# Rolling the TensorE program of a decode layer into a loop, with fixed slots for the K and V loads

## Chip, cores, metric

The kernel runs on one core of a Trainium2 chip. The metric is device microseconds of one execution. All comparisons below are between runs in the fast state, each with runs of the kernel before on the same chip. A ratio is the mean time of one kernel's fast runs over the mean of the other's from the same rounds, so it is not quite the ratio of the medians that are quoted beside it. Beside the experiments the kernel before measured 295.97 to 296.06 us, so medians of different rounds can be compared too.

## The reference

One decode step (one new token, batch 2) of a transformer layer in bf16: layernorm, attention over the last 2048 positions of a K and V cache, out-projection, residual, layernorm, gated FFN, residual.

```python
# D = 640, 32 heads of 192, window W = 2048, FFN width 1536   (cut)
q = (x @ wq).reshape(B, 1, 32, 192).transpose(0, 2, 1, 3)
k = k_cache[:, :, Sk - W:, :]
v = v_cache[:, :, Sk - W:, :]
p = softmax(einsum("bhqd,bhkd->bhqk", q, k) * 192 ** -0.5)
o = einsum("bhqk,bhkd->bhqd", p, v)
h = x + o.reshape(B, 1, 6144) @ wo
out = h + (gelu(ln(h) @ w_gate) * (ln(h) @ w_up)) @ w_down
```

There is almost no reuse: every byte of K and V is used once. The work is 16 groups (4 heads of one batch each), and a group needs one K load and one V load of 3.15 MB each.

## The kernel before

A small recorder collects operations with the tiles that they read and write, works out the waits, and emits one straight-line program for each engine. Loads go into a ring of five slots of 24,576 bytes per partition. They are issued in order, each as soon as the data that it overwrites has been used. For each group TensorE transposes K (12 chunks of 4 transposes), VectorE and ScalarE copy the chunks into `ktr`, and then come scores, softmax and PV.

```python
ring = sb("ring", [128, RING // 2], BF16)          # RING = 5 * 24576
ktr = sb("ktr", [128, 2, 3, 4096], BF16)           # two buffers of transposed K
rq = sb("rq", [128, NG, 6, 16], BF16)              # masked q of all 16 groups

def load(key, nbytes, src, shape):                 # ring position
    if pos[0] + nbytes > RING:
        pos[0] = 0
    off, i = pos[0], pos[1]
    pos[0], pos[1] = off + nbytes, i + 1
    queue.append((key, off, nbytes, src, shape, i))
...
for g in range(NG):                                # order of loads
    if g > 0 and g + 1 < NG:
        load_k(g + 1)
    load_v(g)
    if g % 4 == 3 and g < NG - 5:
        load_wo(g // 4)
load_wo(2); load_wo(3); load_ffn()
...
for g in range(NG):                                # unrolled: 16 groups   (cut)
    transposes(g + 1, 0)
    e_columns(g)
    if J is not None: o_columns(J)                 # every fourth group
    transposes(g + 1, 1)
    if J is not None and J < 2: oproj(J)
    pv(g)
    scores(g + 1)
    softmax(g + 1)
o_rows(3); oproj(2); o_columns(3); oproj(3)        # then layernorm and FFN
```

## Time and profile before

| | before |
|---|---|
| median of 4 runs | 295.99 us (295.89 to 296.05) |
| span of the profiled run | 294.3 us |
| data queue, share of 16 DMA engines | 97.5% |
| TensorE busy | 68% |
| instruction packets (queue q8) | 17, 0.28 MB |

The page's slices (40 equal parts of the span) and its DMA queue table (packets, MB, share of the span of 16 engines):

```profile
PE   2473658848687298849494695858597858586864
DMA  7999999999999999999999999999999999999992
GB/s 268 431 429 445 449 428 426 428 426 424 426 418 433 423 438 431 428 424 438 433 416 446 430 424 423 428 428 430 428 426 431 430 438 423 428 431 411 429 407 113
q1 hardware_dynamic: 6632, 122.29, 97.5%
q8 instruction: 17, 0.28, 0.4%
```

The DMA row is 9 (90% or more) everywhere but in the first and last slice: the loads never pause. TensorE works in bursts.

The waits table (who waited for whom, us in total, times, longest us), and TensorE's timeline for one group (start, us, what):

```profile
PE tps L478 <- DMA ring<-in_A_k_cache_dram: 47.3, 15, 6.9
```

```profile
238.60 4.51 PE L478 MATMUL tps<-identf,ring 128*128 128x128 f32 x24 [3.21 <-DMA ring<-in_A_k_cache_dram]
242.94 0.28 PE L560 MATMUL m<-sel,eexp 128*128 128x64 bf16 x4
243.06 2.82 PE L478 MATMUL tps<-identf,ring 128*128 128x128 f32 x24
245.90 1.49 PE L576 MATMUL ops<-ring,ering 128*32 128x384 bf16 x32
247.21 1.53 PE L534 MATMUL sps<-ktr,rq 128*16 128x512 bf16 x24
249.81 0.18 PE L547 MATMUL m<-mrhs,pm 128*128 128x16 bf16 x1 [1.08 <-DVE mrhs L326]
```

From K's landing at 238.60 to the last matmul at 249.99 a group takes TensorE 11.4 us; the stream brings the next pair of K and V after 14.6 us. So TensorE has about 3 us to spare in a group.

The chain of waits in order of time (start, us, what), its end:

```profile
247.81 29.22 DMA ring<-in_A_wo_dram
...
277.06 0.73 PE m L627 x5
...
291.63 0.33 DVE yrow L748
```

The last piece of `wo` lands at 277.0 us. After it comes a tail of 17.3 us in which out-projection, layernorm and FFN follow one another, while the FFN weights are still arriving. The time is therefore the landing of `wo` plus the tail.

### The profile page before, as it was taken

To read this page: it belongs to the slowest core of one execution; us is meant where nothing else is said; L and a number is where in the kernel's file an instruction comes from. 1 tells how busy PE (TensorE), PEld (TensorE's weight loads), DVE (VectorE), ACT (ScalarE), POOL (GpSimd) and SP (SyncE) were. 2 spreads that over 40 slices of the span, in tenths; PEclk is the share of its full clock that TensorE was granted. 3 is DMA by queue.
4 is the path that set the end of the run, shared out by engine and by line. 5 is a ranking of instruction groups with operands and counts; after the bars stand their busy time and mean duration, and the time that the engine had idled before them with its cause. 6 is when DMAs were issued, how large, how long until landed. Compare 5 with 4: busy or idle time off the path is not lost.

```text
span 294.3 us, 4896 instructions
## 1 busy us (share of the span) xinstructions
PE 198.8 (68%) x2141; PEld 152.4 (52%) x2141; DVE 130.4 (44%) x326; ACT 95.6 (32%) x119; POOL 2.7 (1%) x19
## 2 busy tenths in 40 slices
PE   2473658848687298849494695858597858586864
PEld 1451256728374285637382675655575555553432
DVE  5950366614447054525264343626266526252332
ACT  2150134624332153516151333425254334341000
POOL 3000000000000000000000000000000000000000
PEclk9996579996979589989779697979689979795555
DMA  7999999999999999999999999999999999999992
GB/s 268 431 429 445 449 428 426 428 426 424 426 418 433 423 438 431 428 424 438 433 416 446 430 424 423 428 428 430 428 426 431 430 438 423 428 431 411 429 407 113
DMA packets 6665, 122.61 MB, mean 417 GB/s; under 512 B 754, under 2 KB 756, under 8 KB 1396
## 3 DMA queue, kind: packets, MB, share of 16 engines
q1 hardware_dynamic: 6632, 122.29, 97.5%
q8 instruction: 17, 0.28, 0.4%
q14 instruction: 4, 0.03, 0.0%
q10 hardware_dynamic: 12, 0.00, 0.0%
HBM read 122.29 MB, written 0.00 MB: 416 GB/s over the span
## 4 chain that ended last, share of the span: by engine, by line
DMA 69%; PE 24%; DVE 4%; SPq 1%; issue 1%; ACT 0%; DVEq 0%; ACTq 0%
DMA ring<-in_A_k_cache_dram 50%; PE tps L478 17%; DMA ring<-in_A_wo_dram 10%; DMA ring<-in_A_wq_dram 10%; PE ops L576 1%; DVE rq L330 1%; PE m L627 1%; SPq L271 1%; PE sps L696 1%; PE m L742 1%; PE m L609 1%; PE ops L696 1%; PE tps L707 1%; PE tps L500 1%; PE m L646 0%
## 5 line engine op out<-in xcount | busy, mean ns | idle before, releaser
L478 PE MATMUL tps<-identf,ring 128*128 128x128 f32 x768 | 115.0, 318 | 48.4 <-DMA ring<-in_A_k_cache_dram 47.3
L478 PEld LDWEIGHTS tps<-identf,ring 128*128 128x128 f32 x768 | 106.6, 167 | 51.6 <-DMA ring<-in_A_k_cache_dram 48.7
L487 ACT ACTIVATE ktr<-tps 128x1024 bf16<-128x1024 bf16 x80 | 79.3, 1023 | 88.5 <-PE tps L478 86.9
L490 DVE COPY ktr<-tps 128x1024 bf16<-128x1024 bf16 x112 | 74.2, 688 | 75.7 <-PE tps L478 75.0
L551 ACT ACTIVATE eexp<-sm,nm 128x512 bf16<-128x512 f32 x16 | 11.5, 721 | 64.7 <-DVE nm L549 64.7
L576 PE MATMUL ops<-ring,ering 128*32 128x384 bf16 x512 | 25.0, 339 | 3.6 <-DMA ring<-in_A_v_cache_dram 3.4
L534 PE MATMUL sps<-ktr,rq 128*16 128x512 bf16 x384 | 26.0, 404 | 0.4 <-DVE rq L330 0.4
L540 DVE CUSTOM_DVE_ANT_1 sm<-sps,mska 128x512 f32<-128x512 f32 x16 | 11.1, 691 | 34.1 <-PE sps L534 34.1
L576 PEld LDWEIGHTS ops<-ring,ering 128*32 128x32 bf16 x512 | 12.7, 99 | 12.6 <-DMA ring<-in_A_v_cache_dram 5.6
L534 PEld LDWEIGHTS sps<-ktr,rq 128*16 128x16 bf16 x384 | 9.6, 90 | 11.4 <-issue 2.2
L547 PEld LDWEIGHTS m<-mrhs,pm 128*128 128x128 bf16 x16 | 1.5, 96 | 25.0 <-DVE mrhs L326 25.0
L547 PE MATMUL m<-mrhs,pm 128*128 128x16 bf16 x16 | 2.9, 183 | 16.9 <-DVE mrhs L326 16.9
L500 PE MATMUL tps<-ring,xnT 128*32 128x384 bf16 x80 | 5.7, 444 | 7.6 <-DMA ring<-in_A_wq_dram 7.6
L330 DVE TENSOR_TENSOR rq<-ops,mask 128x96 bf16<-128x96 f32 x16 | 2.7, 250 | 14.6 <-PE ops L518 14.6
L500 PEld LDWEIGHTS tps<-ring,xnT 128*32 128x32 bf16 x80 | 2.4, 119 | 10.4 <-DMA ring<-in_A_wq_dram 8.6
L330 DVE TENSOR_TENSOR ering<-m,mask 128x256 bf16<-128x256 f32 x16 | 6.7, 419 | 2.2 <-PE m L560 2.0
L382 ACT ACTIVATE lt<-m,eps_t 128x2 f32<-128x2 f32 x2 | 0.5, 262 | 20.2 <-PE m L380 20.2
L627 PE MATMUL m<-ring,ot 128*2 128x320 bf16 x96 | 5.7, 379 | 0.3 <-DVE ot L613 0.3
L560 PE MATMUL m<-sel,eexp 128*128 128x64 bf16 x64 | 4.7, 198 | 1.2 <-ACT eexp L551 1.2
L330 DVE TENSOR_TENSOR orow<-m,wm 128x1536 bf16<-128x1536 f32 x3 | 5.3, 1750 | 0.0
L560 PEld LDWEIGHTS m<-sel,eexp 128*128 128x128 bf16 x64 | 4.3, 103 | 1.5 <-DVE nm L549 1.3
L586 DVE COPY osb<-ops 128x192 f32<-128x192 f32 x8 | 2.5, 354 | 5.8 <-PE ops L576 5.8
(112 smaller groups left out, 82.1 us busy)
## 6 DMA issues: line engine op xcount, KB each, us to landing
ring<-in_A_k_cache_dram SPq DMA_DIRECT2D x16, 3072.0 KB, 26.3
ring<-in_A_v_cache_dram SPq DMA_DIRECT2D x16, 3072.0 KB, 29.7
ring<-in_A_wq_dram SPq DMA_DIRECT2D x2, 3072.0 KB, 21.1
ring<-in_A_wo_dram SPq DMA_DIRECT2D x3, 1920.0 KB, 32.2
ring<-in_B_w_gate_dram SPq DMA_DIRECT2D x1, 1920.0 KB, 33.3
ring<-in_B_w_up_dram SPq DMA_DIRECT2D x1, 1920.0 KB, 25.7
ring<-in_B_w_down_dram SPq DMA_DIRECT2D x4, 480.0 KB, 27.6
ring<-in_A_wq_dram SPq DMA_DIRECT2D x1, 1536.0 KB, 28.1
```

The source lines that it names most:

```text
L330: return lambda e: e.tensor_tensor(out=out, in0=a, in1=b, op=op)
L478: ins = e.transpose(tps[bi][:, 128 * u:128 * (u + 1)], kv[:, off:off + 128], identf[:, :])
L487: act(lambda e, dst=dst, bv=bv: e.activation(out=dst, in_=bv, func=ACT.Copy), W=[("kt", slot, n)], X=[("t", bi)])
L490: dve(lambda e, dst=dst, bv=bv: e.tensor_copy(dst, bv), W=[("kt", slot, n)], X=[("t", bi)])
L500: ins = e.matmul(tps[0][32 * r:32 * (r + 1), 0:384], lhsT=xnT[:, c, 32 * J:32 * (J + 1)], rhs=wq[:, c - c0, 1536 * J + 384 * r:1536 * J + ...
L534: ins = e.matmul(sps[32 * ch:32 * ch + 16, :], lhsT=rq[:, g, k, :], rhs=ktr[:, g % 2, k // 2, 1024 * ch + k % 2:1024 * (ch + 1):2], start= ...
L540: dve(lambda e: e.tensor_tensor_reduce(out=sm[:, :].rearrange("p (u x) -> p u x", u=4), in0=sps[:, :].rearrange("p (u x) -> p u x", u=4), ...
L551: act(lambda e: e.activation(out=eexp[:, :], in_=sm[:, :], func=ACT.Exp, bias=nm[:, 0:1], scale=1.0, accum_out=zr[:, g // 4 % 2, g % 4:g % ...
L560: ins = e.matmul(o, lhsT=eexp[:, 128 * u:128 * (u + 1)], rhs=sel64[:, :], start=True, stop=True)
L576: ins = e.matmul(ops_[32 * r:32 * (r + 1), 0:384], lhsT=ering[:, g % 4, t, :], rhs=vv[:, 384 * t:384 * (t + 1)], start=(g % 4 == 0 and t < 4),
L627: ins = e.matmul(m1[32 * r:32 * r + 2, 192:512], lhsT=ot[:, J % 2, kk, :], rhs=wo[:, kk - k0, 320 * h:320 * (h + 1)], start=(kk == 1 or J ...
L696: ins = e.matmul(bank[32 * r:32 * r + 2, 0:384], lhsT=hnT[:, c, :], rhs=wv[:, c, 384 * r:384 * (r + 1)], start=(c == 0), stop=(c == NC5 - ...
```

## The change

It rolls TensorE's program into a loop of 4 trips of 4 groups. The loop as written uses the same addresses in each trip, so the ring gives way to fixed slots (four for K, two for V), the transposed K keeps one buffer, and the masked q of four groups is held at a time and made by GpSimd. A wait inside the loop compares a semaphore with `S * i + a`, where `i` is the trip in a register. The core of the diff (the recorder's bookkeeping is cut):

```diff
-RING = 5 * 24576
+SLOT = 24576
+RING = 6 * SLOT
+K_AT = (0, SLOT, 2 * SLOT, 3 * SLOT)
+V_AT = (4 * SLOT, 5 * SLOT)
+WO_AT = (3 * SLOT, 3 * SLOT, 2 * SLOT, 0)
...
-        ktr = sb("ktr", [128, 2, 3, 4096], BF16)
+        ktr = sb("ktr", [128, 3, 4096], BF16)
-        rq = sb("rq", [128, NG, 6, 16], BF16)
+        rq = sb("rq", [128, 4, 6, 16], BF16)
+        qs = sb("qs", [128, 384], BF16)
...
-            for g in range(NG):            # at the start, on VectorE
-                dve(tt(rq[:, g, ...], ...))
+            dve(lambda e: e.tensor_copy(qs[:, :], ops_[:, 0:384]), W=["qs"], X=["o"])
+            for g in range(4):
+                q_masked(g)                # pool(tt(rq[:, g % 4, ...], ...))
...
             pe(fn, R=[("rq", g % 4)] + [("kt", n) for n in range(12)], X=["s"])   # scores(g)
+            if g + 4 < NG:
+                q_masked(g + 4)
...
+        with eng.Fori(0, trips) as i:
+            ...
+                    for n, o, waits in sorted(bodies.pop(item), key=lambda q: q[0]):
+                        self.emit_one(o, eng, sems, [(key, S * i + a if S else a) for key, a, S in waits])
...
-            P.emit("pe", e, sems)
+            P.emit_loop(e, sems, 4, ["a0", (0, None, ["oc"]), "a1", (0, 3, ["op"]), "a2", "b0", "b1", "b2", "c0", "c1", "c2",
+                                     (None, 3, ["d0", "d1", "d2"])])
```

Bytes and order of the loads stay as they were.

## The prediction

> **What bounds the kernel now.** The DMA stream. The page's slices show DMA share 0.9 or more from the second to the 39th; the queue table gives the data queue 97.5% of 16 engines' span for 122.29 MB. In the windows view each 14.6 us stretch from 44 to 248 us has DMA share 0.99 to 1.01 and about 430 GB/s, with PE busy 7.5 to 12.8 us, mean 10.47. One K and one V (2 x 3.15 MB) take those 14.6 us. TensorE follows: the waits table has it idle 47.3 us for K, 15 times. In the chain of waits the last piece of wo lands at 277.0 us; then out-projection, layernorm and FFN run 17.3 us in latency, while the last FFN weights arrive just in time.

> **What the change does to that.** Bytes, load order and tail stay. Five rotating slots become six fixed ones. By the release conditions, V of group g+2 now needs pv(g) instead of the transposes just before it (1.5 us later), and wo0 and wo1 wait for the transposes of groups 3 and 7 (before, wo0 went out at 61.4 us). At each of these moments two to three transfers of 7.3 us are still queued, 15 to 20 us. The single transposed-K buffer should cost nothing: in TensorE's order scores(g) already precede the transposes of g+1.

> **Costs added on TensorE.** About 20 waits per group become register waits. A stand-alone semaphore instruction on TensorE's queue took 51 ns in this trace; at an estimated two or three such steps per wait that is 2 to 3 us per group, partly hidden behind queued matmuls and evictions. A regular group needs 11.6 us from K's landing to its last small matmul (238.6 to 250.0 in the timeline), one with an out-projection 13.4 (164.1 to 177.6), against 14.6 or more of stream: mostly absorbed. [...] three back-edges and one skip, spread over 250 us, should be recovered from the slack.

> **Gains.** Sixteen DVE multiplies (2.7 us) leave the start; GpSimd does one per group, well ahead of need. The first softmax starts 2 us earlier, but the stream isn't waiting there. Instruction traffic is 0.28 MB, 0.4% in the queue table. If rolling removed three quarters of it, some engines would finish 1 us earlier; if each trip refetches its body, nothing is gained.

> **Critical part.** Almost none: the stream stays saturated, so I expect 295.8 us, 8 in 10 between 294.0 and 298.0. Chances: faster by over 2% 0.01, within 2% 0.95, slower 0.04.

> **What would show it.** DMA share 0.9 or more in all slices from the second to the 39th; TensorE's total wait for K falling from 47 to 15 to 40 us; the last wo piece landing at 277 plus or minus 1.5 us, tail about 17 us; TensorE's busy time unchanged within 3%; the rq multiplies on POOL.

> **What would make it wrong.** Register waits that cost much more than 3 us per group, or that drain the queue before each transposed chunk, so that TensorE needs over 14.6 us per group: then DMA slices drop, the queue's own waits on V slots grow, and the time rises by 16 times the excess. Or back-edge stalls over 15 us, longer than the queued transfers. Or a wait merged over trips that is stricter than the unrolled program's and delays a V or wo load.

The forecast comes to 295.8 us, the 295.99 us measured before with almost nothing taken off. That the back-edges should be recovered from the slack was my estimate. So were the two or three steps in each register wait; the 51 ns for one of them are from the trace.

## The result and the profile after

The changed kernel takes 294.80 us (294.61 to 294.94, 4 runs) against 295.99 us; ratio 0.996, interval 0.9943 to 0.9977. It is 1.2 us faster: clear of noise, well within 2%.

The same parts of the page after the change:

```profile
PE   2573586858677298849493597659696869666764
DMA  7999999999999999999999999999999999999993
GB/s 279 436 427 433 431 440 435 430 425 430 425 420 438 430 433 427 430 430 430 430 421 436 430 430 430 430 430 433 430 430 430 430 430 430 430 430 426 430 406 125
q1 hardware_dynamic: 6632, 122.29, 97.8%
q8 instruction: 7, 0.11, 0.2%
```

The stream is as full as before, and in the second half it is steadier: 430 GB/s in nearly every slice, where before it wandered between 411 and 446. The instruction queue moved 7 packets in place of 17.

The waits table, TensorE's timeline for the same group, and the end of the chain:

```profile
PE tps L549 <- DMA ring<-in_A_k_cache_dram: 45.5, 14, 7.4
```

```profile
237.25 5.38 PE L549 MATMUL tps<-identf,ring 128*128 128x128 f32 x24 [1.84 <-DMA ring<-in_A_k_cache_dram]
242.43 0.42 PE L636 MATMUL m<-sel,eexp 128*128 128x64 bf16 x4
242.66 3.10 PE L549 MATMUL tps<-identf,ring 128*128 128x128 f32 x24
245.69 1.49 PE L652 MATMUL ops<-ring,ering 128*32 128x384 bf16 x32
247.00 1.53 PE L608 MATMUL sps<-ktr,rq 128*16 128x512 bf16 x24
249.61 0.18 PE L623 MATMUL m<-mrhs,pm 128*128 128x16 bf16 x1 [1.08 <-DVE mrhs L398]
```

```profile
248.90 26.84 DMA ring<-in_A_wo_dram
275.78 0.73 PE m L703 x7
...
290.29 0.32 DVE yrow L830
```

The whole gain has arrived when `wo` lands: 275.8 us in place of 277.0. The tail is 293.0 - 275.8 = 17.2 us, as before. Past the first 24 transposes, whose 5.38 us in place of 4.51 may be no more than the granted clock (0.50 in that stretch, 0.62 before), the group is 0.28 us longer (242.63 to 249.79, before 243.11 to 249.99). So the loop's bookkeeping hardly shows. Counted in the trace, TensorE's queue ran 196 register ALU operations (median 32 ns), 19 fused register operations and 19 compare-and-branch (median 77 ns, longest 349 ns) and one move, together 9.7 us of recorded durations in the whole run, or 0.6 us a group; 8.9 of the 9.7 us lay while a matmul was running.

The question is why the same bytes in the same order arrive 1.2 us sooner.

### The profile page after: what moved, and what is told of

It reads as the page before. It is cut to its first block, busy times and chain, and to the rows that moved or that the text cites. A ratio compares the mean times of both kernels' runs of the same rounds, so it can differ in the third digit from the quotient of the medians.

```text
span 293.0 us, 5065 instructions
## 1 busy us (share of the span) xinstructions
PE 198.8 (68%) x2141; PEld 153.0 (52%) x2141; DVE 128.5 (44%) x311; ACT 95.7 (33%) x119; POOL 8.4 (3%) x35
## 3 DMA queue, kind: packets, MB, share of 16 engines
q1 hardware_dynamic: 6632, 122.29, 97.8%
HBM read 122.29 MB, written 0.00 MB: 417 GB/s over the span
## 4 chain that ended last, share of the span: by engine, by line
DMA 72%; PE 23%; SPq 2%; DVE 2%; issue 1%; ACT 0%
DMA ring<-in_A_k_cache_dram 54%; PE tps L549 16%; DMA ring<-in_A_wq_dram 10%; DMA ring<-in_A_wo_dram 9%; SPq L342 2%; PE ops L652 1%; PE m L703 1%; PE m L824 1%; PE sps L778 1%; PE ops L778 1%; PE m L685 1%; PE tps L789 1%; PE tps L571 1%; PE m L722 0%; DVE grow L785 0%
## 5 line engine op out<-in xcount | busy, mean ns | idle before, releaser
L549 PE MATMUL tps<-identf,ring 128*128 128x128 f32 x768 | 116.5, 320 | 46.4 <-DMA ring<-in_A_k_cache_dram 45.5
L652 PE MATMUL ops<-ring,ering 128*32 128x384 bf16 x512 | 24.4, 334 | 4.7 <-DMA ring<-in_A_v_cache_dram 4.7
L616 DVE CUSTOM_DVE_ANT_1 sm<-sps,mska 128x512 f32<-128x512 f32 x16 | 11.1, 691 | 34.9 <-PE sps L608 34.9
L402 POOL TENSOR_TENSOR rq<-qs,mask 128x96 bf16<-128x96 bf16 x16 | 5.6, 359 | 195.9 <-PE sps L608 164.9
L594 DVE CAST qs<-ops 128x384 bf16<-128x384 f32 x1 | 0.6, 558 | 14.4 <-PE ops L589 14.4
L636 PE MATMUL m<-sel,eexp 128*128 128x64 bf16 x64 | 5.3, 213 | 1.2 <-ACT eexp L627 1.2
L636 PEld LDWEIGHTS m<-sel,eexp 128*128 128x128 bf16 x64 | 4.9, 114 | 1.7 <-DVE nm L625 1.3
L703 PE MATMUL m<-ring,ot 128*2 128x320 bf16 x96 | 4.9, 338 | 1.1 <-DMA ring<-in_A_wo_dram 1.1
```

What stands on the lines that cost most here:

```text
L402: return lambda e: e.tensor_tensor(out=out, in0=a, in1=b, op=op)
L549: ins = e.transpose(tps[bi][:, 128 * u:128 * (u + 1)], kv[:, off:off + 128], identf[:, :])
L616: dve(lambda e: e.tensor_tensor_reduce(out=sm[:, :].rearrange("p (u x) -> p u x", u=4), in0=sps[:, :].rearrange("p (u x) -> p u x", u=4), ...
L636: ins = e.matmul(o, lhsT=eexp[:, 128 * u:128 * (u + 1)], rhs=sel64[:, :], start=True, stop=True)
L652: ins = e.matmul(ops_[32 * r:32 * (r + 1), 0:384], lhsT=ering[:, g % 4, t, :], rhs=vv[:, 384 * t:384 * (t + 1)], start=(g % 4 == 0 and t < 4),
L703: ins = e.matmul(m1[32 * r:32 * r + 2, 192:512], lhsT=ot[:, kk, :], rhs=wo[:, kk - k0, 320 * h:320 * (h + 1)], start=(kk == 1 or J < 2 and ...
```

## The experiments

Three theories stood at first. Theory I: fewer instruction packets share the DMA engines with the loads. Theory S: the slots and the order of issue do it. Theory M: the start does it, which VectorE's 16 multiplies no longer fill. A fourth, theory L, came after the first batch: the loop changes the timing of TensorE and so of the releases.

### unrolled and unrolled_dvemask: the change without its loop

```diff
-            P.emit_loop(e, sems, 4, [...])
+            P.emit("pe", e, sems)
```

In the second kernel the masks are also VectorE's again, all 16 at the start.

> The changed kernel with its TensorE program unrolled again; the six fixed slots, the single transposed-K buffer and the GpSimd masks stay. Theory I (the gain of 1.2 us comes from fewer instruction packets on the DMA engines: 17 before, 7 after): the instruction queue is back at about 17 packets and 0.28 MB, ratio to the kernel before 0.999 to 1.001, about 296 us. Theory S (the gain comes from the slots, the order of issue or the masks, not from the loop): 7 or 17 packets, but ratio stays at 0.996, about 294.8 us.

> As unrolled, and the masked q made by VectorE for all 16 groups at the start, as before the change: of the change only the fixed slots and the single buffer are left. Theory I: equal to unrolled within 0.3 us, about 296 us. Theory M (the 2.2 us of VectorE work taken from the start shorten the run): unrolled is near 294.8 and this one near 296 us. The first softmax starts about 2 us later than in unrolled in either case.

Measured: 296.16 us (ratio 1.0004, interval 0.999 to 1.0018) and 296.04 us (1.0001, 0.9987 to 1.0014). The queue table of unrolled:

```profile
q1 hardware_dynamic: 6632, 122.29, 97.6%
q8 instruction: 17, 0.28, 0.4%
```

With the loop taken out, the time and the 17 packets are back. Slots, single buffer and masks are together worth nothing that can be measured, so theories S and M fall. The gain belongs to the loop; what in the loop brings it was still open between I and L.

### fill1 and fill2: more instructions on GpSimd, first attempt

```diff
+            def fn(e):
+                for _ in range(363 if g > 3 else 0):      # fill2: 726
+                    e.nop(nofuse=True)
+                return mul(e)
```

> The changed kernel with 363 no-operations on GpSimd ahead of each of its twelve later masks (4356 in all, about 17 blocks of 16 KB of instructions on an engine that has nothing else to do). Theory I: some 17 more instruction packets than the changed kernel's 7, and about 0.12 us for each, so 296 to 297 us. Theories S and M: 294.8 us, since neither slots, TensorE program nor start differ. The masks must still come in time: no wait of the scores for them beyond the first.

> As fill1 with 726 no-operations a time (8712, about 34 blocks). Theory I: twice the excess of fill1 over the changed kernel, 298 to 299 us, if the packets spread over the engines as before. Theories S and M: 294.8 us.

Measured: 294.92 and 294.90 us, q8 still 7 packets and q14, GpSimd's instruction queue, still 3. This says nothing about theory I: the trace shows only 12 semaphore instructions more on GpSimd's queue, so the no-operations were evidently merged at build time and never fetched. The two runs serve as repeats of the changed kernel.

### loop2x8: a loop whose body is twice as long

```diff
-    P.emit_loop(e, sems, 4, ["a0", ..., (None, 3, ["d0", "d1", "d2"])])
+    P.emit_loop(e, sems, 2, ["a00", ..., "d02", "a10", ..., (None, 1, ["d10", "d11", "d12"])])
```

> The changed kernel's loop as 2 trips of 8 groups in place of 4 trips of 4: same slots, masks and matmuls, and a TensorE program of about 2800 instructions (11 blocks of 256) against about 1790 (7 blocks) in the changed kernel and 4270 (17 blocks) in the kernel before. Theory I (instruction packets): 11 packets if the second trip finds its blocks still in TensorE's instruction memory, up to 19 if it fetches them again; time 294.8 plus 0.12 us for each packet over 7, so about 295.3 us with 11 and 296 us with 17 to 19. Theory L (the loop gains by another timing of TensorE and of the releases, not by traffic): 294.8 us whatever the packets.

Measured: 297.57 us (297.49 to 297.83), ratio 1.0053, interval 1.004 to 1.0066: slower than both kernels, by less than 2% but clear of noise.

```profile
q1 hardware_dynamic: 6632, 122.29, 97.0%
q8 instruction: 21, 0.34, 0.5%
```

A block is what one packet of q8 brings: 16,384 bytes in the records of both kernels, and by the program's counts about 256 instructions (about 1790 in the 7 packets of the changed kernel). This program has 11 such blocks, and 21 packets were moved: the second trip fetched most of its body again. The branch back at 158.0 us took 6.0 us, and nine packets followed between 161.5 and 262.5 us. That stall is not the loss: TensorE had to wait for the next K until 165.4 us anyway. The 4-trip program, some 1790 instructions or 7 blocks, moved 7 packets. Five start by 90.4 us, before its first branch back at 93.6, and the next only at 274.8, so its four trips fetched nothing twice. Theory L (294.8 us for any such loop) fails. Theory I has the sign right but not the size: at 0.12 us for each packet, 21 packets should have cost 1.7 us over the changed kernel, and they cost 2.8 us. The number of packets is not the whole story; the next section finds the rest.

### The lag of the slowest engine

Every load of K, V or weights leaves 16 packets of 4 bytes among the records, and 16 dated increments of its semaphore; the page counts 16 DMA engines. What waits for the load starts after the last increment: in the kernel before, those of the K load that TensorE waits for at 238 us run from 235.21 to 238.55 us, and the transposes start at 238.60. I read each increment as one engine's share being done; the records name no engine. The distance from the first to the last of the 16 is the lag of the slowest engine behind the fastest. Worked out from the increments for the last V load (the packets of 4 bytes carry no load's name and mix two loads where the lag is longer than the distance between them):

```
run               q8 packets   of them before        lag at the last   median time, us
                  in all       the last V lands      V load, us
fill1                  7              5                   2.07             294.92
pework3 (below)        7              5                   2.14             294.95
after                  7              5                   2.21             294.80
fill2                  7              5                   2.33             294.90
before                17             14                   3.36             295.99
unrolled              17             14                   3.38             296.16
unrolled_dvemask      17             14                   3.62             296.04
loop2x8               21             18                   4.97             297.57
```

From after to before the lag grows by 1.15 us and the time by 1.19 us; from after to loop2x8 they grow by 2.76 and 2.77 us. One microsecond of lag costs about one microsecond of time here, because what waits for a load starts after the last of its 16 increments. The fastest engine keeps the same pace: its share of the last K load is done at 249.8 us of the span before, at 249.6 after and at 249.5 in loop2x8. So neither another timing of the releases nor the 6.0 us branch moved the stream. (In unrolled and loop2x8 the chain of waits ends on `w_up`, a few loads after `wo`. The lag delays all of these loads alike.)

The packet records show what delays an engine. A data packet of 24 KB takes 0.91 us as a rule. Between 5 and 256 us of the span, 17 of them took over 1.24 us in the kernel before, 6 after, 16 and 17 in the two unrolled kernels and 19 in loop2x8. Each of these starts within 0.02 us of the end of an instruction packet: in the kernel before 14 after one of q8 and 3 after one of q14, after the change 4 and 2. The pairing is thus seen packet by packet. The costs fit too. A q8 packet takes about 1.05 us, the data packet after it about 0.5 us longer than usual, and one engine's lag grows by about 1.5 us. That the two packets of a pair went through one engine is inferred from this.

The lags also tell where the packets fall, although the increments carry no engine number. In the kernel before, each of TensorE's first eight packets (24.1 to 142.6 us) makes one more of the 16 engines late by about 1.5 us. The ninth, at 168.1 us, is the first to hit a late engine again: the lag jumps from 1.89 us (load complete at 164.1 us) to 3.32 (172.8), and the later ones make more engines late to that degree. In loop2x8 the ninth packet, at 156.6 us, takes the lag from 2.23 to 3.45, and the 17th, at 245.8, from 3.61 to 4.74. So TensorE's packets went round eight engines. The time followed how often one engine was hit (once, twice, three times), not the number of packets. Here lies the size that 0.12 us for each packet missed.

### fillhalf and fillfull: a dose that turned into something else

```diff
+                for k in range(182 if g > 3 else 0):      # fillfull: 363
+                    e.memset(fill[:, k:k + 1], 0)
```

> In place of fill1, whose no-operations were fused and never fetched: 182 one-element memsets on GpSimd ahead of each of its twelve later masks, 2184 instructions or 8.5 blocks, TensorE's loop as in the changed kernel. Theory I: 15 or 16 instruction packets, about 295.8 us. Theory L: 294.8 us.

> As fillhalf with 363 memsets a time, 4356 instructions or 17 blocks. Theory I: 24 packets, about 296.8 us, twice the excess of fillhalf. Theory L: 294.8 us. If the masks come late (wait of the scores for them beyond the first), the run doesn't count.

Measured: 313.32 and 320.12 us (ratios 1.0575 and 1.0794). The groups by line of fillhalf (count, then busy us and mean ns):

```profile
L399 DVE TENSOR_SCALAR mrhs<-oh,mx 128x16 bf16<-128x16 f32 x16 | 64.0, 4002 | 0.6
L631 PE MATMUL m<-mrhs,pm 128*128 128x16 bf16 x16 | 3.1, 191 | 75.0 <-DVE mrhs L399 75.0
```

In the changed kernel the same VectorE operation takes 234 ns. Here it took 4.0 us on average, and the softmax waited for it. The memsets on GpSimd are all that the run adds, so they held VectorE up; by what mechanism, no run here shows. The page's DMA row fell below 9 in five slices between the first and the last. As a test of theory I these runs don't count.

### waitfill2, waitfill4 and waitfill_slow: waits in place of memsets

Semaphore waits that are already met are fetched too (q14 moved 23 packets in waitfill_slow, 3 in the changed kernel), but did not hold VectorE up: in waitfill_slow the operation above takes 234 ns again.

```diff
+                for k in range(300 if g > 3 else 0):      # waitfill2: 728, waitfill4: 1456
+                    e.wait_ge(sems["pe", 0], 1 + k % 2)
...
             P.emit("pool", e, sems)
+            for k in range(1400):                         # waitfill_slow only
+                e.wait_ge(sems["pe", 0], 1 + k % 2)
```

Two such waits become one instruction (the trace of waitfill2 has 4368 for the 8736 written), so these are 364, 728 and 150 instructions a time.

> The changed kernel with 4368 semaphore waits that are already met on GpSimd's queue, 364 ahead of each of its twelve later masks. [...] 0.28 MB of instructions more, in packets of 8 KB as those runs showed for GpSimd: some 34 more packets. Theory I by bytes (0.12 us for 16 KB): 296.8 us, DMA share as before, the last wo piece landing 2 us later. Theory L (the loop's gain is timing, not traffic): 294.8 us. If 294.8 us with the packets counted, then instruction bytes as such are not the cause, but those that TensorE itself waits for or the larger packets.

> As waitfill2 with twice as many, 8736 waits, 0.56 MB, some 68 more packets. Theory I by bytes: 298.9 us, twice the excess of waitfill2. Theory L: 294.8 us.

Measured: 458.19 and 845.94 us. The waits table of waitfill2 shows why these two don't count either:

```profile
PE sps L615 <- POOL rq L402: 178.7, 11, 21.2
```

The masks came late. A wait on GpSimd's queue shows 43 ns in the record but 88 ns from start to start, so 364 of them take 32 us, more than a group. The third kernel was sized by that number.

> As waitfill2, but with as many waits as GpSimd has time for: in waitfill2 a wait on its queue took 88 ns from start to start, so 364 of them held each mask back by 32 us and the scores waited for it. Here 150 ahead of each of the twelve later masks (13 us) and 700 after the last one, 2500 in all, 0.16 MB or some 20 packets of 8 KB. Theory I by bytes (0.12 us for 16 KB): about 296.0 us and the last wo piece 1.2 us later than in the changed kernel. Theory I by packets that hit one engine: up to 297 us. Theory L: 294.8 us. No wait of the scores for the masks beyond the first, or the run doesn't count.

Measured: 305.93 us (305.61 to 306.43), ratio 1.0337, interval 1.0323 to 1.0351. Queue table and slices of waitfill_slow:

```profile
DMA  7999999999999999999999999999999999999900
q8 instruction: 7, 0.11, 0.2%
q14 instruction: 23, 0.19, 0.1%
```

```profile
PE sps L615 <- POOL rq L402: 1.1, 1, 1.1
```

The masks are in time here (one wait of 1.1 us, the first, which the changed kernel has too), TensorE's loop is untouched, and 20 packets of 8 KB more (23 on q14, where the changed kernel has 3) cost 11.1 us, far more than the 1.2 us expected by bytes, and more than the 2 us allowed for packets that hit one engine. The direction is theory I's, and the size has a plain reason in the lags (times of the span):

```
load of waitfill_slow     second-slowest engine   slowest engine   (us behind the fastest)
K of group 4,  80 us             2.07                 2.65
V of group 4, 106 us             2.08                 4.80
V of group 5, 121 us             2.08                 5.25
V of group 6, 136 us             2.10                 5.91
V of group 7, 150 us             2.10                 6.58
last K,       250 us             2.10                11.76
last FFN piece                   1.72                11.83
```

In the changed kernel the slowest engine stays 1.8 to 2.2 us behind from group 2 to the last V load. Here the second-slowest does the same, while a single engine falls back by about 0.65 us with each packet: the packets that GpSimd fetched all delayed the same DMA engine. (A packet of 8 KB takes 0.31 us and the data packet after it 1.26 in place of 0.91, together the 0.65 us.) The last FFN piece is complete at 300.5 us, 10.9 us later than in the changed kernel (289.6). The last slices of the row of GB/s show the wait for that engine:

```profile
GB/s 288 437 415 442 430 422 439 428 414 444 423 414 445 427 415 441 431 422 430 423 435 430 441 421 427 448 415 421 451 421 422 444 427 386 427 414 435 395 35 15
```

A sixteenth of 430 GB/s is 27: in the 39th slice little more than one engine's worth moves.

### pework6 and pework3: how much work TensorE can take

The prediction rests on slack: up to 3 us of TensorE time a group should be absorbed.

```diff
+                    for _ in range(6 if n == 0 and g > 0 else 0):     # pework3: 3
+                        e.matmul(tps[bi][:, :], lhsT=identf[:, :], rhs=kv[:, 0:512], start=True, stop=True)
```

> The changed kernel with six dummy 128x512 float32 matmuls ahead of the first transposes of each group from the second on[...], into a bank that the transposes then overwrite. It tests the prediction's claim that up to 3 us a group is absorbed by the stream: DMA share stays at 0.9 or more, 294.8 to 295.3 us, TensorE's wait for K falls by some 30 us. If the claim is wrong and TensorE's work is on the critical path, up to 40 us more.

> As pework6 with three dummy matmuls. In pework6 the six took 5.4 us of each group by its timeline, not the 2.6 us planned, and a group took up to 16 us against 14.6 of stream; so three are the 2.7 us meant to test the claim that up to 3 us a group is absorbed. Claim right: 294.6 to 295.4 us, DMA share 0.9 or more to the end, wait for K some 35 us shorter than in the changed kernel. Claim wrong: 299 us or so, half of pework6's excess.

Measured: pework6 303.97 us (ratio 1.0284, interval 1.0265 to 1.0303), pework3 294.95 us (0.9968, 0.9954 to 0.9983). TensorE's timeline of pework6, one group:

```profile
212.46 5.41 PE L548 MATMUL tps<-ring,identf 128*128 128x512 f32 x12
217.71 2.78 PE L551 MATMUL tps<-identf,ring 128*128 128x128 f32 x24
...
228.08 0.18 PE L625 MATMUL m<-mrhs,pm 128*128 128x16 bf16 x1 [0.22 <-DVE mrhs L398]
228.55 5.41 PE L548 MATMUL tps<-ring,identf 128*128 128x512 f32 x12 [0.28 <-issue]
```

The dummies took 5.4 us, twice the 2.6 us planned, and the group 228.55 - 212.46 = 16.1 us. TensorE no longer waits for K: it runs from group to group, so it has become the limit. With half the dose nothing is lost: pework3 is as fast as the changed kernel, and its DMA row stays at 9 from the second to the 39th slice. The dose did arrive: in the group that starts at 208 us, K's landing to the last small matmul takes 14.9 us in place of 12.2. TensorE's wait for K fell from 45.5 to 26.2 us, less than the 35 us expected. So the slack is real, and it ends between these two doses.

## Why the prediction was right

- **The DMA stream bounds the kernel, and the change hardly touches it.** Right. Predicted 295.8 us with 294.0 to 298.0; measured 294.80. The DMA row is 9 from the second to the 39th slice in both kernels.
- **Slots, single buffer and masks cost and bring nothing.** Right, and shown: unrolled and unrolled_dvemask equal the kernel before to within 0.2 us.
- **Up to 3 us of TensorE work a group is absorbed.** Right: pework3 lengthens a group by 2.7 us (14.9 in place of 12.2) and loses nothing, pework6 adds 5.4 us a group and loses 9 us. But the loop never needed that slack.
- **The register waits cost 2 to 3 us a group.** Wrong in size. The register and branch instructions took 0.6 us a group. So the wait for K did not fall to 15 to 40 us, as I had named for a sign; it went from 47.3 to 45.5 us.
- **Back-edges fetch code again and stall, to be recovered from the slack.** Not shown by any trace when it was written, and not what happened in this kernel. Seven packets were moved for seven blocks of program, so no trip fetched anything again; the three branches back, at 93.6, 156.7 and 220.1 us, took 0.21 to 0.24 us, and the longest branch took 0.35 us. In loop2x8 it did happen: 21 packets were moved for 11 blocks, the branch back took 6.0 us, and the wait for K absorbed it. So a body of about 1010 instructions (the difference of the two looped programs, 2800 and 1790) stayed from trip to trip, and one of about 2020 did not. Where the limit lies between them, no run here shows.
- **Instruction traffic: some engines finish 1 us earlier if three quarters of it go.** Right in kind, and this is the whole gain: packets went from 17 to 7, the slowest engine's lag from 3.36 to 2.21 us, the landing of `wo` from 277.0 to 275.8 us. But I had put this down as an if and left it out of the central figure, which is why that is 1 us high.

## What to carry to other kernels

In this kernel, whose loads keep all 16 DMA engines busy (97.5% of their span), the time followed the slowest engine, not the mean share: 1.15 us of lag cost 1.19 us. Look at instruction packets in the queue table even when they are 0.4% of the engines' time, ask how often they hit the same engine, and roll a long program if its body stays resident: the body that stayed took 294.80 us here, no loop 295.99, and the body that was fetched again 297.57. Before costing loop overhead from guesses, count it: here it was 0.6 us a group against 3 us of slack.
